# One decode block on one core: the second gate/up round and eight down row chunks in two whole loads, four single chunks at the end

## The chip, the core and the metric

The kernel runs on one core of one Trainium2 chip. The metric is the device time of one execution in microseconds (us), the median of several runs. In this document TensorE is the matrix engine (PE in the profile, its weight loads PEld), VectorE is DVE, ScalarE is ACT, GpSimd is POOL and SyncE is SP; SPq and ACTq are the queues from which SP and ACT issue transfers (DMAs).

## The reference

One token for each of eight sequences goes through an attention sublayer on cached keys and values and then through a gated feed-forward block, all in float32:

```python
W = 1024                                   # last W of 4096 cached positions
q = layernorm(x) @ wq                      # x: 8 x 1024, 32 heads of 128
p = softmax(q . k * 128 ** -0.5)           # 4 key/value heads, 8 query heads each
h = x + (p . v) @ wo
n = layernorm(h)
out = h + (gelu(n @ w_gate) * (n @ w_up)) @ w_down     # 1024 -> 3584 -> 1024
```

All weights and the cache window are read once: some 111 MB.

## The kernel before

All weights pass through one SBUF region, `space`, of 128 KB per partition, seen as two buffers `wbuf[0]` and `wbuf[1]` of 64 KB per partition each (8192 KB over 128 partitions). The loads alternate between the buffers: two for wq, two for the keys, two for the values, two for wo, then the gate and up weights. Every load is one DMA, issued by SP in program order through `move` (line 91) with the semaphore of the last matmul that still reads the place. SP waits in order, so an issue that waits holds back every issue behind it.

Each weight matrix is used with a batch of 8 on the narrow side. A matmul takes 32 stationary columns (four copies of the 8 rows) against 512 moving columns, and its result goes to 32 of the 128 PSUM partitions; the four partition quarters are the four **column groups** j, and matmuls on different groups run side by side. A float32 matmul appears in the trace as two records, each with its weight load.

The feed-forward block has two rounds, `SETS = (4, 3)`: round 0 covers 4 column groups of 512 of the 3584 hidden columns, round 1 the other 3. For each round k, s = 0 is the gate and s = 1 the up product (line 376): a loop over the eight 128-row slices c and, inside, over the groups j. After the gate ScalarE applies gelu (L386), after the up VectorE multiplies (`hm`, L389), TensorE transposes (L188, L397), and VectorE writes the transposed hidden rows to `at` (L400), from which the down product takes its stationary operand.

Round 0 loads into the two whole buffers. Round 1 has two loads of 6144 KB, which lie one behind the other at the front of `space`: the gate load waits for `used[0, 0]` (the end of round 0's gate products), the up load for `half_used` (half of round 0's up products). `place` and `base` are the end of them: 24 rows of 1024 per partition out of 32.

The down weights are 28 row chunks q of 128 x 1024. They come in `PARTS = (8, 8, 4, 4, 2, 1)` chunks per load and then the last one, 27, in two column pieces `ENDS = (128, 128)` of each quarter of 256. The first eight (4096 KB) go to the free quarter of `space` after `used[0, 1]`; chunks 8 to 15 and 16 to 19 wait for `used[1, 0]`, all others for `used[1, 1]`. Between these two issues stand the eight small `side` loads (line 436), which bring 320 columns of chunk 19 in another layout.

TensorE multiplies chunks pair by pair into `ya` (L461): two chunks by two halves of 512 columns on the four groups. Chunk pair 16 (`SLOW`) uses two groups only. `first = 28 - TAIL` is where this ends; with `TAIL = 2` it covers chunks 0 to 25. Then VectorE copies `ya` to `d1` (L474). Chunk 26 is multiplied in another form, by `add` (L483): each group takes one quarter of 256 output columns, in two halves in the banks `acc` and `tb`. After it `add` folds `d1` into the same banks with the constant `add2`. The two pieces of chunk 27 follow (L495), each as its load lands; ScalarE copies each half to `o_fin` (L498), and two DMAs write the result, one issued by SP and one by ACT.

Of the kernel before, what the change touches and what calls it, by code (L numbers as in the profile page):

```python
# [7 lines left out]
P = 128  # L8
B = 8
D = 1024  # L10
# [4 lines left out]
NC = D // P  # L15
# [3 lines left out]
N = 512  # L19
# [8 lines left out]
SIDE = 19  # L28
SIDE_COLS = 320
SIDE_ROWS = (0, 16, 64, 80)  # L30
ENDS = (128, 128)
TAIL = 2


SLOW = range(16, 18)
# [2 lines left out]
class Flow:  # L38
# [50 lines left out]
    def move(self, name, out, src, *waits, engine="sync"):  # L89
        s = self.sem(name)  # L90
        self.start(engine, lambda e: e.dma_start(out, src), waits).then_inc(s, 16)  # L91
        return s, 16


def decode_block(nc, x, wq, kt, v, wo, gu, dn, side, ends, outs):
# [14 lines left out]
    def sb(name, *shape):  # L110
        return nc.alloc_sbuf_tensor(name, list(shape), F32).ap()
# [243 lines left out]

    at = sb("at", P, DF // P, 32)
    at_ok = []
    q0 = 0  # L360
# [2 lines left out]
    for k, nb in enumerate(SETS):  # L363
        pair = big[1 - k].rearrange("p (s n) -> p s n", s=2)
        clear = (ps[1][1], h_ok)[k]
        for s in range(2):
            if k == 0:
                w, w_in, wb = load(gu[k][s], f"gu{k}_{s}", "c n", c=NC)
            else:
                n = NC * nb * N  # L370
                w = space[:, place:place + n].rearrange("p (c n) -> p c n", c=NC)
                w_in = move(f"gu{k}_{s}", w, gu[k][s], (used[0, 0], half_used)[s])
                place += n
            for c in range(NC):
                for j in range(nb):
                    tok = run("tensor", lambda e: e.matmul(  # L376
                        pair[32 * j:32 * j + 32, s, :], ht[c], w[:, c, j * N:(j + 1) * N],
                        start=(c == 0), stop=(c == NC - 1)),
                        w_in, ht_ok, clear, mark=(c in (NC // 2 - 1, NC - 1) and j == nb - 1))
                if (k, s, c) == (0, 1, NC // 2 - 1):  # L380
                    half_used = tok
            used[k, s] = tok
            if s == 0:
                rows = 32 * nb
                ge = sb(f"ge{k}", P, N)
                g_ok = run("scalar", lambda e: e.activation(  # L386
                    ge[:rows], pair[:rows, 0, :], AF.Gelu_apprx_tanh), tok)
        hm = sb(f"hm{k}", P, N)
        tok = run("vector", lambda e: e.tensor_mul(hm[:rows], ge[:rows], pair[:rows, 1, :]), tok, g_ok)  # L389
        hp, tok = transposes(ta, hm[:rows], N // P, tok, ta_free, rows)  # L390
        if k == 1:

            g, i = divmod(SIDE - q0, N // P)
            sp = ta[0:48, N - 32 * len(SIDE_ROWS):N].rearrange("p (s m) -> p s m", m=32)
            assert g == 0 and rows * (N // P) + 32 * len(SIDE_ROWS) <= N
            for s, c0 in enumerate(SIDE_ROWS):
                tok = run("tensor", lambda e: e.transpose(  # L397
                    sp[:, s, :], hm[0:32, i * P + c0:i * P + c0 + 48], ident[0:32, 0:32]),
                    mark=(s == len(SIDE_ROWS) - 1))
        ta_free = run("vector", lambda e: e.tensor_copy(  # L400
            at[:, q0:q0 + nb * (N // P), :].rearrange("p (j i) m -> p i j m", j=nb),
            hp.rearrange("p i (j m) -> p i j m", j=nb)), tok)
        at_ok.append(ta_free)
        if k == 1:
            at_side = sb("at_side", 48, len(SIDE_ROWS), 32)
            side_ok = run("scalar", lambda e: e.copy(at_side, sp), ta_free)
        q0 += nb * (N // P)
# [11 lines left out]
    def rows_of(q):  # L419
        return ring[:, slot(q)]  # L420

    arrived = {}
    q0 = 0
    for i, n in enumerate(PARTS):


        a, b = slot(q0), slot(q0) + n
        clear = used[0, 1] if a >= base else used[1, 0] if b * D <= place // 2 else used[1, 1]
        assert b <= SLOTS and (a >= base or b <= base)
        if q0 <= SIDE < q0 + n:  # L430
            assert SIDE == q0 + n - 1

            side_in = fl.sem("w_side")
            for h, src in enumerate(side):
                p0 = h % 4 + 32 * (h // 4)
                fl.start("sync", lambda e: e.dma_start(w_side[p0:p0 + 13:4], src), [zero[-1]]).then_inc(
                    side_in, 16)
            side_in = side_in, 16 * len(side)
            here = move(f"wd{i}", space[:, a * D:b * D - SIDE_COLS], dn[i], clear)
        else:  # L440
            here = move(f"wd{i}", ring[:, a:b], dn[i], clear)
        arrived.update((q, here) for q in range(q0, q0 + n))
        q0 += n
# [35 lines left out]
    def add(lhs, rhs, *waits, start=False):  # L479

        for d_ps, a, b in halves:
            for j in range(NQ):
                run("tensor", lambda e: e.matmul(  # L483
                    d_ps[32 * j:32 * j + 32, :], lhs(j), rhs(j)[:, a:b], start=start, stop=False),
                    *waits, mark=False)

    for q in range(first, last):
        add(lambda j: at[:, q, :], lambda j: rows_of(q)[:, j * QW:(j + 1) * QW], arrived[q], at_ok[1],
            start=(q == first))
    add(lambda j: add2[:, j // 2, :], lambda j: d1[:, (j % 2) * QW:(j % 2) * QW + QW], d1_ok)  # L490
    o_fin = sb("o_fin", P, QW)
    done = []
    for (c0, n, t, here), (d_ps, a, b) in zip(blocks, halves):
# [107 lines left out]
```

## Time and profile before

| | |
|---|---|
| median of 3 runs | 265.2 us (265.1 to 265.26) |
| the profiled execution, whole | 265.43 us |
| its span in the trace | 264.1 us |
| mean granted TensorE clock | 0.774 of full speed |
| TensorE matmuls busy | 139.8 us, 53% of the span |
| VectorE, ScalarE, GpSimd busy | 23.3, 10.9 and 5.5 us |
| DMA | 111.44 MB, mean 422 GB/s |

Times in the rows are us from the start of the span unless marked ns. A row of the timeline gives start and length of a merged group, engine, line, operation, output and inputs with their shape, the count, and in brackets the idle time of that engine before it and what ended it. A row of the chain of waits gives start, length and what ran or was waited for. In tables by stretch the columns are the stretch, its length, busy time and count of PE, PEld, DVE, ACT and POOL, the granted TensorE clock (1.00 is 2.4 GHz, 0.50 is 1.2 GHz), the busy share of the 16 DMA engines and GB/s. In a list of DMA issues the last number is the time from issue to landing.

### The profile page before, as it was taken

The page shows a single profiled execution, that of the slowest core. Times are in us where ns is not written, and L with a number is a line of the kernel's source. Part 1 is how long each engine was busy: PE and PEld are TensorE (multiplying, and loading weights), DVE is VectorE, ACT ScalarE, POOL GpSimd, SP SyncE. Part 2 cuts the span into 40 slices and gives each one's busy share as a digit, 9 for nine tenths or more (in the row PEclk, how much of TensorE's full clock was granted, in tenths as well). Part 3 has the DMA queues.
Part 4 walks back from the last instruction along what each step waited for, and adds up shares of the span by engine and source line. Part 5 has one row for each costly group of instructions (what it writes and reads, how often), then busy time and mean ns, then how long its engine had stood idle before and what let it go on. Part 6 is the DMA issues. An engine that isn't in the chain of part 4 may idle for free.

```text
span 264.1 us, 2071 instructions
## 1 busy us (share of the span) xinstructions
PE 139.8 (53%) x958; PEld 40.4 (15%) x958; DVE 23.3 (9%) x55; ACT 10.9 (4%) x17; POOL 5.5 (2%) x15
## 2 busy tenths in 40 slices
PE   0015805805905806806707808818509677587596
PEld 0011201201201301302202202112102111122122
DVE  0320100100020110200200100160000200010001
ACT  1010000000010010110000000020000000000000
POOL 8000000000000000000000000000000000000000
PEclk9999985985865975975955956965955959599599
DMA  8997999999799989989998999999999989999995
GB/s 318 481 457 338 476 476 390 407 467 477 328 476 467 439 367 457 469 347 477 447 457 367 479 437 437 397 437 477 390 407 439 477 387 442 412 442 432 402 413 191
DMA packets 3256, 111.44 MB, mean 422 GB/s; under 512 B 392, under 2 KB 648, under 8 KB 1072
## 3 DMA queue, kind: packets, MB, share of 16 engines
q1 hardware_dynamic: 3088, 111.22, 98.0%
q8 instruction: 7, 0.11, 0.2%
q10 hardware_dynamic: 160, 0.10, 0.1%
q14 instruction: 1, 0.01, 0.0%
HBM read 111.18 MB, written 0.13 MB: 422 GB/s over the span
## 4 chain that ended last, share of the span: by engine, by line
DMA 78%; PE 20%; SPq 0%; issue 0%; ACT 0%
DMA w<-gu 20%; DMA w<-wq 16%; DMA w<-v 11%; DMA w<-kt 11%; DMA w<-wo 11%; DMA w<-dn 9%; PE big L376 6%; PE tb L233 4%; PE tb L308 4%; PE ya L336 3%; PE big L261 3%; SPq L91 0%; PE acc L483 0%; ACT o_fin L498 0%; PE tb L483 0%
## 5 line engine op out<-in xcount | busy, mean ns | idle before, releaser
L376 PE MATMUL big<-w,ln_t 128*32 128x512 f32 x224 | 37.8, 758 | 19.8 <-DMA w<-gu 19.8
L336 PE MATMUL ya<-w,ot 128*32 128x512 f32 x128 | 18.9, 755 | 18.8 <-DMA w<-wo 18.8
L261 PE MATMUL big<-w,qz 128*32 128x512 f32 x128 | 18.0, 724 | 19.3 <-DMA w<-kt 19.3
L461 PE MATMUL ya<-w,at 128*32 128x512 f32 (+1 forms) x104 | 16.1, 695 | 4.6 <-DMA w<-dn 4.6
L376 PEld LDWEIGHTS big<-w,ln_t 128*32 128x32 f32 x224 | 9.2, 135 | 47.0 <-issue 26.7
L308 PE MATMUL tb<-w,pt 128*32 128x512 f32 x64 | 9.5, 757 | 9.4 <-DMA w<-v 9.4
L233 PE MATMUL tb<-w,ln_t 128*32 128x512 f32 x64 | 9.5, 762 | 8.9 <-DMA w<-wq 8.9
L308 PE MATMUL acc<-w,pt 128*32 128x512 f32 x64 | 8.9, 719 | 10.0 <-DMA w<-v 10.0
L233 PE MATMUL acc<-w,ln_t 128*32 128x512 f32 x64 | 8.9, 720 | 7.5 <-DMA w<-wq 7.5
L188 PE MATMUL ta<-ident,ln_xn 64*128 64x64 f32 x16 | 2.2, 318 | 19.4 <-DVE ln_xn L214 19.4
L336 PEld LDWEIGHTS ya<-w,ot 128*32 128x32 f32 x128 | 5.2, 135 | 31.0 <-issue 31.0
L261 PEld LDWEIGHTS big<-w,qz 128*32 128x32 f32 x128 | 4.7, 130 | 31.9 <-issue 22.3
L389 DVE TENSOR_TENSOR hm<-ge,big 128x512 f32<-128x512 f32 (+1 forms) x2 | 1.4, 686 | 56.7 <-PE big L376 56.7
L461 PEld LDWEIGHTS ya<-w,at 128*32 128x32 f32 x104 | 3.8, 124 | 15.7 <-issue 8.7
L270 DVE TENSOR_REDUCE nmax<-big 128x1 f32<-128x1024 f32 x2 | 2.4, 1224 | 33.9 <-PE big L261 33.9
L272 ACT ACTIVATE p<-big,nmax 128x1024 f32<-128x1024 f32 x2 | 2.2, 1114 | 76.6 <-DVE nmax L270 76.6
L308 PEld LDWEIGHTS tb<-w,pt 128*32 128x32 f32 x64 | 2.6, 134 | 15.6 <-issue 15.6
L188 PEld LDWEIGHTS ta<-ident,ln_xn 64*128 64x128 f32 x16 | 1.9, 216 | 20.3 <-DVE ln_xn L214 20.3
L308 PEld LDWEIGHTS acc<-w,pt 128*32 128x32 f32 x64 | 2.5, 130 | 15.8 <-issue 15.8
L233 PEld LDWEIGHTS tb<-w,ln_t 128*32 128x32 f32 x64 | 2.3, 135 | 15.5 <-DMA w<-wq 9.1
L233 PEld LDWEIGHTS acc<-w,ln_t 128*32 128x32 f32 x64 | 2.5, 130 | 13.2 <-issue 13.2
L205 ACT ACTIVATE ln_sd<-ln_ve 64x1 f32<-64x1 f32 x2 | 0.4, 203 | 69.4 <-DVE ln_ve L204 69.4
(81 smaller groups left out, 53.3 us busy)
## 6 DMA issues: line engine op xcount, KB each, us to landing
w<-gu SPq DMA_DIRECT2D x2, 6144.0 KB, 23.5
w<-dn SPq DMA_DIRECT2D x2, 4096.0 KB, 26.6
w<-dn SPq DMA_DIRECT2D x1, 2048.0 KB, 19.9
w<-dn SPq DMA_DIRECT2D x1, 1888.0 KB, 23.6
w<-dn SPq DMA_DIRECT2D x1, 1024.0 KB, 22.0
w<-dn SPq DMA_DIRECT2D x1, 512.0 KB, 22.7
w<-ends SPq DMA_DIRECT2D x2, 256.0 KB, 23.0
w_side<-side SPq DMA_DIRECT2D x8, 20.0 KB
```

The source lines that it names most:

```text
L188: tok = run("tensor", lambda e, i=i: e.transpose(t[:, i, :], src[:, i * P:(i + 1) * P], ident[:rows, :rows]), id_ok, ready, clear, mark=(i ...
L205: tok = run("scalar", lambda e: e.activation(sd, ve, AF.Sqrt), tok)
L233: tok = run("tensor", lambda e, c=c, j=j: e.matmul(q_ps[32 * j:32 * j + 32, :], xt[c], w[:, c, j * N:(j + 1) * N], start=(c == 0), stop=(c ...
L261: tok = run("tensor", lambda e: e.matmul(s_ps[32 * r:32 * r + 32, k0:k0 + N], qz[hf][:, s, c0:c0 + 32], k_t[:, s, half * HB + b, k0:k0 + N ...
L270: tok = run("vector", lambda e: e.tensor_reduce(out=nmax, in_=s_ps, axis=AX.X, op=ALU.max, negate=True), tok)
L272: p_ok = run("scalar", lambda e: e.activation(p_sb, s_ps, AF.Exp, bias=nmax, accum_out=tot), tok)
L308: tok = run("tensor", lambda e: e.matmul(o3[32 * r:32 * r + 32], pt[:, c, 32 * r:32 * r + 32], v_t[:, s, c, half * HB:(half + 1) * HB, :], ...
L336: tok = run("tensor", lambda e: e.matmul(ya[32 * r:32 * r + 32, :], ot[:, 2 * hf * REP + h + e2].rearrange("p r b -> p (r b)"), w[:, h + e ...
L376: tok = run("tensor", lambda e: e.matmul(pair[32 * j:32 * j + 32, s, :], ht[c], w[:, c, j * N:(j + 1) * N], start=(c == 0), stop=(c == NC ...
L389: tok = run("vector", lambda e: e.tensor_mul(hm[:rows], ge[:rows], pair[:rows, 1, :]), tok, g_ok)
L461: tok = run("tensor", lambda e: e.matmul(ya[32 * r:32 * r + 32, 0:n], at[:, q + e2, :], rows_of(q + e2)[:, ch * N:ch * N + n], start=(q == ...
```

## The change

Round 1 and the first eight down chunks are laid out together in DRAM, 128 KB per partition, as [gate | up | chunks 0 to 7], and loaded by two DMAs of 8192 KB, `whole[0]` into `wbuf[0]` after `used[0, 0]` and `whole[1]` into `wbuf[1]` after `used[0, 1]`. `whole[0]` holds the gate weights and the first eight of the 24 (c, j) blocks of up: all of c = 0 and 1, and j = 0, 1 of c = 2. `whole[1]` holds the other 16 and the eight chunks. Every place in `space` stays what it was. `half_used` and the separate load of chunks 0 to 7 are gone. A product of round 1 now waits for the whole load in which its block lies.

The order of round 1's products changes. The gate goes over all three groups for c = 0 to 3, over groups 0 and 1 for c = 4 to 7, and then over c = 4 to 7 on group 2. The up products of c = 0 to 2 go group by group, the others as before; the ninth of them, (2, 2), is the first that needs `whole[1]`.

`TAIL` becomes 4: the pairs in `ya` end with chunk 23, and chunks 24, 25 and 26 are multiplied in the form of `add`. The copy to `d1` follows chunk 23, and the fold of `d1` stands ahead of chunk 24. `ENDS` becomes (160, 96). All loads from chunk 8 on keep their sizes, order and waits, except the two pieces of chunk 27.

```diff
-ENDS = (128, 128)
-TAIL = 2
+ENDS = (160, 96)
+TAIL = 4
...
+    def order(k, s):
+        if (k, s) == (1, 1):
+            return [(c, j) for j in range(3) for c in range(3)] + \
+                [(c, j) for c in range(3, NC) for j in range(3)]
+        if (k, s) == (1, 0):
+            return [(c, j) for c in range(NC) for j in range(3 if c < NC // 2 else 2)] + \
+                [(c, 2) for c in range(NC // 2, NC)]
+        return [(c, j) for c in range(NC) for j in range(SETS[k])]
...
-                w_in = move(f"gu{k}_{s}", w, gu[k][s], (used[0, 0], half_used)[s])
+                if s == 0:
+                    whole = [move(f"whole{i}", wbuf[i], src, used[0, i]) for i, src in enumerate(gu[k])]
                 place += n
...
+            for c, j in order(k, s):
+                if k == 1:
+                    w_in = whole[(place - n + (c * nb + j) * N) // BUF]
+                tok = run("tensor", lambda e: e.matmul(
+                    pair[32 * j:32 * j + 32, s, :], ht[c], w[:, c, j * N:(j + 1) * N],
+                    start=(c == 0), stop=(c == NC - 1)),
+                    w_in, ht_ok, clear, mark=((c, j) == order(k, s)[-1]))
...
-    arrived = {}
-    q0 = 0
-    for i, n in enumerate(PARTS):
+    q0 = SLOTS - base
+    arrived = {q: whole[1] for q in range(q0)}
+    for i, n in enumerate(PARTS[1:], 1):
...
-        clear = used[0, 1] if a >= base else used[1, 0] if b * D <= place // 2 else used[1, 1]
+        clear = used[1, 0] if b * D <= place // 2 else used[1, 1]
...
+    add(lambda j: add2[:, j // 2, :], lambda j: d1[:, (j % 2) * QW:(j % 2) * QW + QW], d1_ok,
+        start=True)
     for q in range(first, last):
-        add(lambda j: at[:, q, :], lambda j: rows_of(q)[:, j * QW:(j + 1) * QW], arrived[q], at_ok[1],
-            start=(q == first))
-    add(lambda j: add2[:, j // 2, :], lambda j: d1[:, (j % 2) * QW:(j % 2) * QW + QW], d1_ok)
+        add(lambda j: at[:, q, :], lambda j: rows_of(q)[:, j * QW:(j + 1) * QW], arrived[q], at_ok[1])
```

## Rows read from the trace of the kernel before

**Rows 1.** Page, DMA queues: packets, MB, share of 16 engines over the span

```profile
q1 hardware_dynamic: 3088, 111.22, 98.0%
```

**Rows 2.** Chain of waits in time: start, length, what it was

```profile
90.58 30.26 DMA w<-v
...
130.45 29.14 DMA w<-wo
...
168.62 29.89 DMA w<-gu
...
205.10 22.48 DMA w<-gu
...
237.56 22.74 DMA w<-dn
```

**Rows 3.** Timeline of TensorE and its weight loads, round 1

```profile
213.09 9.46 PE L376 MATMUL big<-w,ln_t 128*32 128x512 f32 x48 [3.08 <-DMA w<-gu]
...
218.52 0.12 PEld L376 LDWEIGHTS big<-w,ln_t 128*32 128x32 f32 x3 [0.31 <-issue]
...
227.62 9.02 PE L376 MATMUL big<-w,ln_t 128*32 128x512 f32 x48 [5.08 <-DMA w<-gu]
```

**Rows 4.** Timeline of TensorE, ahead of the second layernorm

```profile
169.47 1.90 PE L347 MATMUL big<-y_sb,to_rows 128*64 128x512 f32 x4 [0.90 <-DVE y_sb L344]
```

**Rows 5.** Timeline of SP, the issues around the change

```profile
222.98 5.08 SPq L436 DMA_DIRECT2D w_side<-side  x8
228.10 9.89 SPq L91 DMA_DIRECT2D w<-dn  x4
238.03 0.91 SPq L91 DMA_DIRECT2D w<-ends  x2
```

**Rows 6.** Stretches of 1 us: busy times, granted clock, DMA share, GB/s

```profile
204.00:205.00 1.00, 1.00 (x12) 0.24 (x8) 0.00 (x0) 0.00 (x0) 0.00 (x0) 0.85 0.23 98
...
224.00:225.00 1.00, 0.00 (x0) 0.00 (x0) 0.00 (x0) 0.00 (x0) 0.00 (x0) 0.89 0.34 147
231.00:232.00 1.00, 1.00 (x9) 0.31 (x6) 0.00 (x0) 0.00 (x0) 0.00 (x0) 0.70 1.22 524
245.00:246.00 1.00, 0.00 (x0) 0.00 (x0) 0.00 (x0) 0.00 (x0) 0.00 (x0) 0.63 0.99 415
```

**Rows 7.** Timeline of TensorE, down chunks 0 to 23

```profile
238.70 4.01 PE L461 MATMUL ya<-w,at 128*32 128x512 f32 x30
...
247.05 8.69 PE L461 MATMUL ya<-w,at 128*32 128x512 f32 x48 [4.34 <-DMA w<-dn]
...
255.66 1.27 PE L470 MATMUL ya<-w_side,at_side 48*32 48x320 f32 x8
...
256.86 1.92 PE L461 MATMUL ya<-w,at 128*32 128x512 f32 x16
```

**Rows 8.** List of DMA issues: KB each, us from issue to landing

```profile
w<-dn SPq DMA_DIRECT2D x1, 1888.0 KB, 23.6
...
w<-ends SPq DMA_DIRECT2D x2, 256.0 KB, 23.0
...
out<-o_fin ACTq DMA_DIRECT2D x1, 64.0 KB, 1.6
```

**Rows 9.** Timeline of all engines, the end

```profile
260.22 0.69 DVE L474 COPY d<-ya 128x512 f32<-128x512 f32 x1 [21.33 <-PE ya L461]
...
260.97 0.43 PE L483 MATMUL acc<-d,add 128*32 128x128 f32 x8
...
261.65 0.40 PE L495 MATMUL tb<-w,at 128*32 128x128 f32 x8
...
262.12 0.27 ACT L498 COPY o_fin<-tb 128x128 f32<-128x128 f32 x1
...
262.41 0.35 ACTq L91 DMA_DIRECT2D out<-o_fin  x1
```

**Rows 10.** Stretch of 1 us while the result is written, columns as above

```profile
263.00:264.00 1.00, 0.00 (x0) 0.00 (x0) 0.00 (x0) 0.00 (x0) 0.00 (x0) 1.00 0.44 131
```

More of the change, by code (lines that the diff above doesn't have):

```diff
@@ L371, in decode_block @@
                 w = space[:, place:place + n].rearrange("p (c n) -> p c n", c=NC)
-                w_in = move(f"gu{k}_{s}", w, gu[k][s], (used[0, 0], half_used)[s])
+                if s == 0:
+                    whole = [move(f"whole{i}", wbuf[i], src, used[0, i]) for i, src in enumerate(gu[k])]
                 place += n
[L374 to L381, printed above, removed]
+            for c, j in order(k, s):
[5 more added lines that the diff above has]
+                    w_in, ht_ok, clear, mark=((c, j) == order(k, s)[-1]))
             used[k, s] = tok
@@ L420, in rows_of @@
         return ring[:, slot(q)]
-    arrived = {}
-    q0 = 0
-    for i, n in enumerate(PARTS):
+    q0 = SLOTS - base
+    arrived = {q: whole[1] for q in range(q0)}
+    for i, n in enumerate(PARTS[1:], 1):
         a, b = slot(q0), slot(q0) + n
-        clear = used[0, 1] if a >= base else used[1, 0] if b * D <= place // 2 else used[1, 1]
-        assert b <= SLOTS and (a >= base or b <= base)
+        clear = used[1, 0] if b * D <= place // 2 else used[1, 1]
+        assert b <= base
         if q0 <= SIDE < q0 + n:
@@ L540 @@
     for nb in SETS:
-        for m in (B_w_gate, B_w_up):
-            gus.append(m[:, f0:f0 + nb * N].reshape(NC, P, nb * N).transpose(1, 0, 2).reshape(-1))
+        gus.append([m[:, f0:f0 + nb * N].reshape(NC, P, nb * N).transpose(1, 0, 2).reshape(P, -1)
+                    for m in (B_w_gate, B_w_up)])
         f0 += nb * N
@@ L545 @@
     at = [sum(PARTS[:i]) for i in range(len(PARTS))]
+    both = np.concatenate(gus[1] + [rows[:PARTS[0]].transpose(1, 0, 2).reshape(P, -1)], 1)
+    gus[1] = [both[:, :NC * SET], both[:, NC * SET:]]
     width = [n * D - (SIDE_COLS if a <= SIDE < a + n else 0) for a, n in zip(at, PARTS)]
@@ L548 @@
         rows[a:a + n].transpose(1, 0, 2).reshape(P, -1)[:, :m].reshape(-1)
-        for a, n, m in zip(at, PARTS, width)])
+        for a, n, m in list(zip(at, PARTS, width))[1:]])
     side = np.stack([
@@ L562 @@
         "x": own(A_x).reshape(B, D), "wq": own(wq), "kt": own(kt), "v": own(v), "wo": own(wo),
-        "gu": np.concatenate(gus), "dn": dn, "side": own(side), "ends": ends,
+        "gu": np.stack([own(g) for k in gus for g in k]), "dn": dn, "side": own(side), "ends": ends,
     }
@@ L577 @@
     flat, f0 = aps["dn"], 0
-    aps["dn"] = []
-    for n, m in zip(PARTS, width):
+    aps["dn"] = [None]
+    for n, m in list(zip(PARTS, width))[1:]:
         t = flat[f0:f0 + P * m]
@@ L584 @@
     aps["side"] = [aps["side"][i] for i in range(8)]
-    flat, f0 = aps["gu"], 0
-    aps["gu"] = []
-    for nb in SETS:
-        size = P * NC * nb * N
-        aps["gu"].append([
-            flat[f0 + i * size:f0 + (i + 1) * size].rearrange("(p c n) -> p c n", p=P, c=NC)
-            for i in range(2)
-        ])
-        f0 += 2 * size
+    aps["gu"] = [[aps["gu"][2 * k + i] for i in range(2)] for k in range(2)]
+    aps["gu"][0] = [g.rearrange("p (c n) -> p c n", c=NC) for g in aps["gu"][0]]
     decode_block(nc, outs=outs, **aps)
```

## Prediction, written before the changed kernel ran

> **What bounds the kernel now.** I read the DMA queues first. The one queue that carries the weights occupies the 16 DMA engines for 98.0% of the span [rows 1], while TensorE is busy for 53%. Then I read the chain of waits in time, because a share over the whole span doesn't tell which wait ends last. There each load takes over where the one before ended: landings (start plus length) at 120.84, 159.59 and 198.51, each after two loads of 8192 KB, at 227.58 after two of 6144 KB, and at 260.30 [rows 2]. Matmuls appear on this chain only in the time in which the next load was running anyway. So the kernel is a stream of loads with a short tail: the last piece of chunk 27 lands at about 238.5 + 23.0 = 261.5 [rows 5, 8], and the span ends at 264.1. A change can gain in three ways: bytes move faster, the tail behind 261.5 gets shorter, or a place where the stream ran dry is filled. It loses if TensorE or a late issue falls behind the stream.
>
> **Two loads in place of three.** The bytes stay the same, so only a cost per load can be saved. Two 8192 KB loads took 38.75 and 38.92 us, two 6144 KB loads 29.07 us [rows 2]; three quarters of the former are 29.06 to 29.19. A fixed cost per load is therefore nil as far as these rows can tell. Chunks 0 to 15 (two loads of 4096 KB) took 247.05 - 227.58 = 19.47 us up to the matmuls that waited for them [rows 2, 7], as one load of 8192 KB does. The three loads thus took 29.07 + 9.73 = 38.80, and two whole ones would take 38.75 to 38.92: a gain of 0.05 to a loss of 0.12. I take 0.
>
> **Are the loads issued in time?** `whole[0]` waits as the gate load did. `whole[1]` waits for all of round 0's up products rather than half: these start at 198.56, and sixteen record rounds of 0.43 us, the first 5.7 us of them at half clock, end them at 208.3 (the clock was half until 204.3, see below). It is needed when `whole[0]` has landed, 198.51 + 19.4 = 217.9, so 9 us are in hand. `whole[1]` lands at 237.3. Before, chunks 8 to 15 were issued just ahead of 222.98, where the side loads begin on SP [rows 5]; they wait for the end of the gate products, which moves (next part) to 230.2 to 231.1, 6 us before they are needed. Behind that wait on SP stand eight side issues (5.08 us), chunks 16 to 19 and then the wait for the up products (next part: 242.4) with chunks 20 to 27 behind it. Chunk 19 lands at 228.10 + 23.6 = 251.7 [rows 5, 8], so these have 9 us in hand too. All of it is hidden; were one cover gone, the price would be the lateness plus at most the 1.6 us that a small transfer took from issue to landing [rows 8].
>
> **Round 1 on TensorE.** With full clock a record of 512 columns takes 0.12 + 0.31 = 0.43 us per group [rows 3], so a product (two records) takes 0.86, for up to four groups side by side; at half clock twice that. Four records in a row on the same groups with changing weights took 1.90 us, that is 4 x 0.43 and a drain of some 0.2 [rows 4]: work on one group costs time in proportion and no more. Where the clock stands I read from stretches of 1 us: 0.85 in the one from 204 puts a rise at 204.3, 5.7 us after the products began at 198.56; 0.70 from 231 puts one at 231.6, 4.0 us after 227.62 [rows 3, 6]. Falls: 0.89 from 224 is a fall at 224.8, 2.2 us after matmuls ended (222.55); 0.63 from 245 is one at 245.3, 2.55 us after 242.71 [rows 3, 6, 7].
>
> The gate goes from 8 steps of 0.86 to 12: four on three groups, four on two, four on one. Starting at 217.9 with a clock that rises after 4.0 to 5.7 us, it takes 12 x 0.86 + 2.0 to 2.85 = 12.3 to 13.2 us and ends at 230.2 to 231.1 (before: 9.46). The eight up products from `whole[0]` go group by group; where one group's last meets the next group's first they overlap, so they make 6 steps, 5.1 us, to 235.3 to 236.2. TensorE then idles 1.1 to 2.0 us until 237.3. That is less than the 2.2 and 2.55 us after which the clock was seen to fall, so I expect the other 16 up products at full clock: one alone and five steps of three, 5.1 us, to 242.4. Before, the up products ended at 236.64; from there multiply, transposes, and chunks 0 to 7 ended at 242.71, 6.07 us later [rows 3, 7]. So these end at 248.5. Chunks 8 to 15 (since 247.05) take four steps, 3.4 us, to 251.9; before, they began at half clock. Pair 16 on two groups 1.71, pair 18 0.86 and the side products 1.27 [rows 7] end at 255.7. Before, the side products ended at 256.93 and chunks 20 to 23 began right there [rows 7]. Those have landed by 256.6 to 256.86; the row before doesn't show the landing, since TensorE was later, and I take 256.6. The reordering itself so costs nothing at the end: it lies in time in which TensorE had waited 5.08 and 4.34 us [rows 3, 7]. Without that cover its cost would be 6 steps, 5.1 us.
>
> **The tail.** Chunks 20 to 23 end at 256.6 + 1.92 = 258.5 [rows 7], the copy to `d1` (0.69, and 0.06 to start [rows 9]) at 259.3. Nothing of TensorE hides this copy now; before, chunk 26 did. Then come the fold and chunks 24, 25 and 26: a quarter-form chunk streams four records of a quarter length, 0.43 us, as a chunk in `ya` does, so these end at 259.3 + 4 x 0.43 = 261.05. Loads 24 to 26 (all in by 260.30 [rows 2]) don't hold them up. The 160-column piece of chunk 27 takes 0.27 to 261.3, and the 96-column piece then starts when it lands, at 261.5. Before, it started at 261.65, behind the fold that had waited for `d1` to 260.97 [rows 9]: 0.15 gained. Its matmuls stream 32 columns less, four records of 0.43 x 32/512 over two passes: some 0.05 of their 0.40; ScalarE's copy of 0.27 and its DMA lose about 0.03 together. The rest, copy, issue and 1.6 us of landing, stays. Sum: 0.15 + 0.05 + 0.03 = 0.23 us.
>
> The smaller write could cost instead: its rows are 384 B, where 512 B were. The engines were busy for 0.44 us with both halves [rows 10], so twice the time for one half is at most 0.2 us more. The Trainium skill (DMA: Bandwidth & Descriptors, Specifications) says that below 512 B a DMA engine reads, modifies and writes. By that rule the gain would be used up; no row here has such a write. I take 0 and keep 0.2 for the range.
>
> **The sum** is made against the profiled execution: 265.43 - 0.23 = 265.2. The median, 265.2, lies 0.23 under that execution, so a median of 265.0 is my forecast, with 264.8 to 265.3 for this case. About 0.2% (0.53 us) is what a measurement of this kernel can tell from no change.
>
> **Rivals.**
>
> *The clock falls in the gap before `whole[1]`.* The idle time of up to 2.0 us is close to 2.2. If the clock rises early, the first eight end early and the gap is longest. The remaining products and the chain behind them would then run partly at half clock: from about 237.4 until 4.0 to 5.7 us after 237.3, some 3.5 to 5.5 us, which costs 1.7 to 2.7. Chunks 20 to 23 would begin at 257.4 to 258.4 rather than 256.6. In the chain from there (1.92, 0.75, five steps to the last piece) nothing waits, so the last piece starts 0.5 to 1.5 later than before: 265.6 to 266.6 as a median, of which I take 265.7, since overlap of the side products with the next chunks shortens it. For it: every earlier pause fell to 0.50. Against it: those were all longer. Half of its cases stay within 0.2%.
>
> *One group doesn't keep the clock up (slower).* If the one-group stretch of the gate, from 226.7 on, and the eight up products don't hold the clock as four groups do, it falls 2 us or more into that stretch. The eight up products then take 10.3 us, to 241.3, past the landing of `whole[1]`, and the rest starts cold: up products to some 248.5 rather than 242.4, and after the 1 us in hand the end is up to 5 us later, 265.5 to 270, with 267.5 as the middle. It decides once the granted clock falls between 226 and 237. For it: no row shows a stretch of several us on one group. Against it: three groups let the clock rise at 231.6 as four did at 204.3 [rows 6], and the stretch with pair 16 on two groups ran on at full clock behind 252.
>
> *A saved load saves time (faster by more than 0.2%).* If each load had a fixed cost of about 2 us on the stream, one load less would give 263.0. The Trainium skill (DMA: Bandwidth & Descriptors, Anatomy of one DMA) puts such a fixed part of about 2.0 us on each DMA of another issuing path. Here the next load is queued long before the last ends, and rows 2 leave nothing of it.
>
> *The change does nothing that shows.* The last landing, the copies and the write decide, and 0.23 us goes in the 96-column write: 265.2.
>
> **How the numbers follow.** Forecast 0.47; clock falls in the gap 0.25; one group doesn't hold the clock 0.14; a saved load 0.04; nothing shows 0.10. Faster by over 0.2%: 0.05 (the saved load and a sliver of the forecast). Slower: 0.12 + 0.14 = 0.26. Within: 0.69. The range runs from 264.7 to 266.3: it leaves out the saved load and most of the one-group case, some 0.16.
>
> **What would show each step.** Landings of `whole[0]` and `whole[1]` near 217.9 and 237.3; the gate ending near 230.5; full clock from about 222 to 237 and beyond; the side products ending before 256.6; the fold starting near 259.3 and the last piece at its landing, 261.5. I am wrong if the clock drops before 237, if chunks 20 to 23 start later than 257, or if the stream ends before 261.3.

## Result and the profile after

| | before | changed |
|---|---|---|
| median | 265.2 us (6 runs, 265.1 to 265.31) | 266.62 us (6 runs, 265.93 to 267.11) |
| profiled execution, whole | 265.43 us | 266.54 us |
| its span | 264.1 us | 265.0 us |

The ratio is 1.005 with a 95% interval of 1.004 to 1.006: the change makes the kernel slower by half a per cent, where 265.0 had been forecast and a time above 266.3 had been left out. The executions of the changed kernel also spread over 1.2 us, those before over 0.2. Between the medians the loss is 1.42 us, between the two profiled executions 1.1; the traces account for the 0.9 by which their spans differ.

The chain of waits of the changed kernel, in time (start, length, what it was), the counterpart of [rows 2]:

```profile
208.20 28.83 DMA w<-gu
...
237.07 7.50 PE big L390 x32
...
247.16 9.44 PE ya L473 x75
```

Before, the chain ran over the loads to 260.30 [rows 2]. Now the last load on it lands at 237.03 (the second whole load; 208.20 + 28.83), and from there on TensorE alone carries it: up products, chunks, the copy to `d1`, the quarter steps, without any wait for data. TensorE has become the bound of the last 28 us. The last piece of chunk 27 lands at 261.4 (see the loads, below) and waits 1.1 us until TensorE takes it up at 262.51.

The timeline of TensorE, VectorE and ScalarE, for [rows 3, 7, 9]:

```profile
217.67 12.23 PE L390 MATMUL big<-w,ln_t 128*32 128x512 f32 x64 [7.99 <-DMA w<-gu]
...
228.13 0.59 ACT L398 ACTIVATE ge<-big 96x512 f32<-96x512 f32 x1 [39.20 <-PE big L390]
...
237.07 7.48 PE L390 MATMUL big<-w,ln_t 128*32 128x512 f32 x32 [7.17 <-DMA w<-gu]
...
246.59 10.01 PE L473 MATMUL ya<-w,at 128*32 128x512 f32 x78
...
256.53 1.27 PE L482 MATMUL ya<-w_side,at_side 48*32 48x320 f32 x8
...
257.73 1.92 PE L473 MATMUL ya<-w,at 128*32 128x512 f32 x16
...
259.72 0.69 DVE L486 COPY d<-ya 128x512 f32<-128x512 f32 x1 [12.95 <-PE ya L473]
...
260.47 0.48 PE L495 MATMUL acc<-d,add 128*32 128x160 f32 x8 [0.81 <-DVE d L486]
...
262.51 0.35 PE L507 MATMUL tb<-w,at 128*32 128x96 f32 x8
```

The timeline merges the gate and the eight up products of the first whole load into one row: they take 12.23 us and end at 229.90; the gate's gelu starts at 228.13. TensorE then waits 7.17 us. The other 16 up products take 7.48. Chunks 0 to 19 follow without a pause, the side products end at 257.80, chunks 20 to 23 start at 257.73 (256.86 before), and the last piece at 262.51 (261.65 before). That 0.86 us is the span's 0.9.

The granted clock in stretches of 1 us (the third number from the right), for [rows 6]:

```profile
220.00:221.00 1.00, 1.00 (x6) 0.19 (x3) 0.00 (x0) 0.00 (x0) 0.00 (x0) 0.52 1.66 721
230.00:231.00 1.00, 0.00 (x0) 0.00 (x0) 0.00 (x0) 0.00 (x0) 0.00 (x0) 1.00 1.51 655
234.00:235.00 1.00, 0.00 (x0) 0.00 (x0) 0.00 (x0) 0.00 (x0) 0.00 (x0) 0.80 0.68 295
236.00:237.00 1.00, 0.00 (x0) 0.00 (x0) 0.00 (x0) 0.00 (x0) 0.00 (x0) 0.50 1.22 524
241.00:242.00 1.00, 1.00 (x9) 0.28 (x6) 0.00 (x0) 0.00 (x0) 0.00 (x0) 0.78 1.14 492
```

It rises at 220.95 (0.52 in the first row), holds through the gate and the first up products, falls at 234.6, 4.7 us after they ended, and is at 0.50 when the second load lands. It rises again at 241.4, 4.4 us after the work began.

### The profile page after: what moved, and what is told of

It is laid out like the page before. It is cut to its first block, busy times and chain, and to the rows that moved or that the text cites. A ratio compares the mean times of both kernels' runs of the same rounds, so it can differ in the third digit from the quotient of the medians.

```text
span 265.0 us, 2118 instructions
## 1 busy us (share of the span) xinstructions
PE 137.5 (52%) x982; PEld 41.3 (16%) x982; DVE 23.3 (9%) x55; ACT 10.9 (4%) x17; POOL 5.5 (2%) x15
## 4 chain that ended last, share of the span: by engine, by line
DMA 71%; PE 27%; DVE 1%; issue 0%; ACT 0%; SPq 0%; DVEq 0%
DMA w<-gu 22%; DMA w<-wq 15%; DMA w<-kt 11%; DMA w<-wo 11%; DMA w<-v 11%; PE big L390 7%; PE ya L473 4%; PE big L261 4%; PE tb L233 4%; PE tb L308 4%; PE ya L336 3%; PE acc L495 0%; PE ya L482 0%; PE ya L465 0%; DVE d L486 0%
## 5 line engine op out<-in xcount | busy, mean ns | idle before, releaser
L390 PE MATMUL big<-w,ln_t 128*32 128x512 f32 x224 | 38.7, 745 | 27.3 <-DMA w<-gu 27.3
L261 PE MATMUL big<-w,qz 128*32 128x512 f32 x128 | 19.2, 766 | 19.8 <-DMA w<-kt 19.8
L390 PEld LDWEIGHTS big<-w,ln_t 128*32 128x32 f32 x224 | 9.9, 133 | 54.8 <-issue 27.5
L473 PE MATMUL ya<-w,at 128*32 128x512 f32 (+1 forms) x96 | 12.4, 589 | 0.0
L233 PEld LDWEIGHTS tb<-w,ln_t 128*32 128x32 f32 x64 | 2.3, 135 | 15.5 <-DMA w<-wq 9.3
L398 ACT ACTIVATE ge<-big 128x512 f32<-128x512 f32 (+1 forms) x2 | 1.2, 594 | 51.8 <-PE big L390 51.8
```

The costliest lines, as they stand in the source:

```text
L233: tok = run("tensor", lambda e, c=c, j=j: e.matmul(q_ps[32 * j:32 * j + 32, :], xt[c], w[:, c, j * N:(j + 1) * N], start=(c == 0), stop=(c ...
L261: tok = run("tensor", lambda e: e.matmul(s_ps[32 * r:32 * r + 32, k0:k0 + N], qz[hf][:, s, c0:c0 + 32], k_t[:, s, half * HB + b, k0:k0 + N ...
L390: tok = run("tensor", lambda e: e.matmul(pair[32 * j:32 * j + 32, s, :], ht[c], w[:, c, j * N:(j + 1) * N], start=(c == 0), stop=(c == NC ...
L398: g_ok = run("scalar", lambda e: e.activation(ge[:rows], pair[:rows, 0, :], AF.Gelu_apprx_tanh), tok)
L473: tok = run("tensor", lambda e: e.matmul(ya[32 * r:32 * r + 32, 0:n], at[:, q + e2, :], rows_of(q + e2)[:, ch * N:ch * N + n], start=(q == ...
```

## Experiments

**1. The tail alone.** The kernel before, with its three loads and its order of round 1.

```diff
-ENDS = (128, 128)
-TAIL = 2
+ENDS = (160, 96)
+TAIL = 4
...
+    add(lambda j: add2[:, j // 2, :], ..., d1_ok, start=True)
     for q in range(first, last):
-        add(..., start=(q == first))
-    add(lambda j: add2[:, j // 2, :], ..., d1_ok)
+        add(...)
```

> The kernel before with only the tail of the change: four single chunks, the fold ahead of them, pieces of 160 and 96 columns; three loads as before. Theory A (TensorE comes late and cold out of the gap ahead of the second whole load; the tail is no cause of its own): chunks 20 to 23 start at about 256.9 as before, end at 258.8, the copy to d1 at 259.55, and five quarter steps of 0.43 put the last piece at 261.6; span 263.9 to 264.1, median 265.0 to 265.3. Theory B (the copy to d1, which nothing on TensorE hides any more, costs the time by itself): the last piece starts 0.7 to 0.9 us later than 261.65, median 265.9 to 266.2.

Measured: 265.36 us (10 runs), before 265.24; ratio 1.0002 [0.9993, 1.0012]. The timeline of its end:

```profile
256.33 1.92 PE L461 MATMUL ya<-w,at 128*32 128x512 f32 x16
...
258.33 0.69 DVE L474 COPY d<-ya 128x512 f32<-128x512 f32 x1 [20.11 <-PE ya L461]
...
259.07 0.48 PE L483 MATMUL acc<-d,add 128*32 128x160 f32 x8 [0.81 <-DVE d L474]
...
261.30 0.37 PE L495 MATMUL tb<-w,at 128*32 128x96 f32 x8
```

Between 258.33 and 259.07 TensorE waits for the copy, and that costs nothing: four more steps follow, and the last piece starts at 261.30, when it has landed (261.26 in the trace). Theory B falls. The 0.23 us forecast for the tail don't show in the median either.

**2. The loads and the order alone**, with the tail of before.

```diff
-ENDS = (160, 96)
-TAIL = 4
+ENDS = (128, 128)
+TAIL = 2
```

and `add` for the fold behind chunk 26 again.

> The changed kernel with the tail of before: two whole loads and the new order of round 1, TAIL = 2, fold behind chunk 26, pieces of 128 and 128. Theory A: the up products still run partly at half clock from 237.1 to about 244.5, chunks 20 to 23 still start near 257.7 and end at 259.65; chunks 24 and 25 follow at once to 260.5, the copy ends at 261.25 beside chunk 26, fold 0.43, last piece at about 262.0 where the changed kernel had 262.51: span 264.4 to 264.6, median 265.8 to 266.2. So about half a microsecond of the loss would belong to the tail on top of a late TensorE. Theory B: back to 265.1 to 265.4.

Measured: 266.22 us (10 runs, 265.23 to 266.4); ratio 1.0027 [1.0014, 1.004].

```profile
236.92 7.92 PE L390 MATMUL big<-w,ln_t 128*32 128x512 f32 x32 [6.74 <-DMA w<-gu]
...
258.01 2.78 PE L473 MATMUL ya<-w,at 128*32 128x512 f32 x24
...
260.87 0.69 DVE L486 COPY d<-ya 128x512 f32<-128x512 f32 x1 [13.81 <-PE ya L473]
...
262.29 0.40 PE L507 MATMUL tb<-w,at 128*32 128x128 f32 x8
```

The up products start at half clock (7.92 us in all), TensorE is late at 258.01, and the last piece starts at 262.29. So the loads and the order make the kernel slower by themselves. The median lies just above the 265.8 to 266.2 of theory A, and the executions fall into two sets: three at 265.23 to 265.48, as before, and seven at 266.04 to 266.4, of which the profiled one (266.04) is one. Against the changed kernel this one is some 0.4 us faster at the median, and its trace is 0.5 us shorter from the start of chunk 20 to the last piece (258.01 to 262.29, there 257.73 to 262.51): with a late TensorE the copy to `d1`, here beside chunk 26, is no longer free in the new tail.

**3. The plain order of round 1** in the changed kernel.

```diff
     def order(k, s):
-        if (k, s) == (1, 1):
-            return ...
-        if (k, s) == (1, 0):
-            return ...
         return [(c, j) for c in range(NC) for j in range(SETS[k])]
```

> The changed kernel with round 1's products in the plain order, all groups inside every c, for gate and up. Theory A (matmuls on different groups run beside each other whatever their order, so the new order hardly lengthens the work): the products of the first whole load end at 228.5 to 229.5 where they ended at 229.9, the clock falls before 237, the up products end at 244 to 245, median 266.2 to 267.1, as the changed kernel. Theory C (the new order is itself the loss, because it delays the end of the gate or leaves groups idle): median below 266.0.

Measured: 266.4 us (5 runs, 265.85 to 267.15); ratio 1.0048 [1.0029, 1.0067], the changed kernel's.

```profile
217.72 11.24 PE L384 MATMUL big<-w,ln_t 128*32 128x512 f32 x64 [8.00 <-DMA w<-gu]
...
237.16 7.46 PE L384 MATMUL big<-w,ln_t 128*32 128x512 f32 x32 [8.21 <-DMA w<-gu]
```

The products of the first load end at 228.96 where they end at 229.90 with the new order, and the second load finds the clock low either way. Theory C, a median below 266.0, falls. The new order lengthened TensorE's work by 1 us, not by the 5 to 6 that the forecast gave it.

**4. Eight extra products on the idle fourth group** fill the gap. They write to `ya`, which is begun anew later.

```diff
             for c, j in order(k, s):
+                if (k, s, c, j) == (1, 1, 2, 2):
+                    for g in [3] * 8:
+                        run("tensor", lambda e: e.matmul(
+                            ya[32 * g:32 * g + 32, :], ht[0], w[:, 0, 0:N], start=True, stop=True),
+                            ya_free, mark=False)
```

> The changed kernel with eight extra products on the idle fourth column group, into the bank ya that is written anew later, between the last up product of the first whole load and the first of the second; they read data that is there and change nothing in the result. One of them takes 0.86 us at full clock, all 6.9. Theory A: TensorE is busy to 236 or later, the clock stays at 1.00, the up products take 5.1 to 5.6 us and end at 242.2 to 242.8 in place of 244.55, chunks 20 to 23 start when they have landed (256.5), the last piece at its landing (261.45): span 263.7 to 264.0, median 265.0 to 265.3. Rival (work on one group doesn't hold the clock): it falls before 237 in spite of the products, and the median stays at 266.3 or more.

Measured: 265.29 us (10 runs, 265.06 to 266.28); ratio 1.0011 [1.0001, 1.0022]; profiled span 263.8.

```profile
230.32 5.74 PE L390 MATMUL ya<-w,ln_t 128*32 128x512 f32 x13
...
237.29 5.34 PE L395 MATMUL big<-w,ln_t 128*32 128x512 f32 x32 [1.23 <-DMA w<-gu]
...
256.43 1.92 PE L478 MATMUL ya<-w,at 128*32 128x512 f32 x16 [0.56 <-DMA w<-dn]
```

and the clock in it:

```profile
235.00:236.00 1.00, 1.00 (x3) 0.11 (x1) 0.00 (x0) 0.00 (x0) 0.00 (x0) 1.00 0.08 33
236.00:237.00 1.00, 0.06 (x1) 0.00 (x0) 0.00 (x0) 0.00 (x0) 0.00 (x0) 1.00 1.14 492
```

TensorE works until 236.06, from 230.32 on with the extra products alone, on one group of four, and the clock stays at 1.00 through the remaining gap of 1.23 us. The up products take 5.34 us in place of 7.48, and chunks 20 to 23 wait for their load again. This is the loss of the changed kernel, taken back by nothing but a warm clock. The rival that one group doesn't hold the clock falls with it. Four of the ten executions still took 265.5 or more; experiments 8 and 9 are about these.

**5. The step in dispute, measured by itself:** sixteen extra products, four on each group, written group by group.

```diff
-                    for g in [3] * 8:
+                    for g in sorted(list(range(4)) * 4):
```

> The changed kernel with sixteen extra products at the same place, four on each column group, written group by group: four on group 0, then four on 1, 2 and 3. They go into ya and change nothing in the result. It measures the step on which the forecast's gap stood. In order, one group's run beside the next only where they meet (the forecast's reckoning): 13 steps of 0.86 us, 11.1 us, so TensorE is busy from 229.9 to about 241 and the up products of the second load start 4 us late. All groups beside each other whatever the order: 4 steps, 3.4 us, so it ends at about 233.3 and idles until 237. A queue of a few matmuls per group would lie between: 5 to 9 us.

Measured: one execution, 265.01 us, span 263.7.

```profile
228.79 0.59 PE L390 MATMUL ya<-w,ln_t 128*32 128x512 f32 x1
...
229.65 7.98 PE L390 MATMUL ya<-w,ln_t 128*32 128x512 f32 x30
```

The first starts at 228.79, the last ends by 237.63 (229.65 + 7.98): 8.8 us, between the 11.1 of strict steps and the 3.4 of free groups. The starts of the records in the trace tell how: each group's first record begins 1.75 us, four records, after the first of the group before, when that one has two products left. So in this order a group begins once the run ahead of it has two products to go, and a run of n products takes n - 2 steps, the last run n.

**6. Pair 16 on four groups.**

```diff
-SLOW = range(16, 18)
+SLOW = ()
```

> The changed kernel with chunk pair 16 on four column groups in place of two. Theory A (TensorE is late and every step behind the second load counts): pair 16 takes 0.86 in place of 1.71 us, chunks 20 to 23 start 0.8 us earlier, at 256.8 to 256.9, the last piece at 261.5 to 261.7; median 265.6 to 265.9 where the changed kernel had 266.62. If TensorE's lateness isn't the cause, no difference: 266.3 or more.

Measured: 265.61 us (10 runs, 264.98 to 266.22); ratio 1.0011 [1.0, 1.0021]. In the profiled execution (265.97):

```profile
247.10 9.15 PE L473 MATMUL ya<-w,at 128*32 128x512 f32 x78
```

The median falls by one microsecond for 0.86 us of TensorE time taken out behind the second load (9.15 in place of 10.01): it was on the path. In this execution the clock rose at 242.45, later than in the changed kernel's, so that the last piece started at 262.16 and not at the 261.5 to 261.7 expected.

**7. Nine extra products and pair 16 on four groups.**

> The changed kernel with nine extra products on the fourth column group (as eight before) and chunk pair 16 on four groups. Theory A: TensorE is busy until about 236.9, the clock holds in every execution, TensorE waits for chunks 20 to 23 by a microsecond or more, and the end is set by the last landing alone: median 265.0 to 265.2 with a spread of no more than the kernel before, 0.1 to 0.2 below it at best, since what lies behind the last landing is only some 0.2 us shorter. If the tail costs something of its own, it stays at 265.4 or more.

Measured: 265.31 us (12 runs, 264.88 to 268.37); ratio 1.0022 [0.9996, 1.0048]. The median lies 0.1 above the 265.0 to 265.2 expected and below the 265.4 of the other reading. The spread was not expected: four executions took 266.7 to 268.4. The profiled one (265.35) was not of these, so the trace doesn't show them:

```profile
256.31 1.93 PE L478 MATMUL ya<-w,at 128*32 128x512 f32 x16 [1.41 <-DMA w<-dn]
```

Here TensorE waited 1.41 us for chunks 20 to 23, and the granted clock stayed at 1.00 until after the end of the work. Two causes that the next experiments show could both act in the four, an eighth instruction load and a clock lost through this wait; which it was stays open.

**8. Four extra products** on the fourth group in place of the eight of experiment 4, with the tail of the change.

> The changed kernel with four extra products on the fourth column group in place of eight: they end at about 232.6 and leave a gap of 4.4 us ahead of the second load. Theory A: the clock falls in that gap in most executions (falls were seen 2.2 and 2.55 us after work had ended) and the time is that of the changed kernel or a little less, 266.0 to 266.8. If the mere presence of extra products helped, or one group's work counted in another way, the time would be half way or better, below 265.8.

Measured: 266.89 us (4 runs); ratio 1.0049 [1.0034, 1.0063]. The time is 0.1 above the expected range, and not for the expected reason alone. The clock fell at 236.5, just ahead of the load, and TensorE ended 0.8 us earlier than in the changed kernel (262.07 against 262.86). What took the time is the write of the result. The page's row of the instruction queue (packets, MB, share), and the issues of the write (KB, us to landing):

```profile
q8 instruction: 8, 0.13, 0.2%
```

```profile
out<-o_fin SPq DMA_DIRECT2D x1, 80.0 KB, 3.1
...
out<-o_fin ACTq DMA_DIRECT2D x1, 48.0 KB, 3.2
```

There are eight instruction loads here, seven before and in the changed kernel, and the write takes 3.1 and 3.2 us in place of 1.6 [rows 8]. The 16 more TensorE instructions of this kernel brought it. The packets in the trace show how it delayed the write: it ran from 263.26 to 264.43, and 16 of the write's 256 packets, the share of one of the 16 DMA engines, began only at 264.43, while all others were done by 263.77. So the run doesn't tell how much four products help. Experiments 4, 5 and 7 have eight loads too; in their profiled executions the additional one came between 260.8 and 262.6, ahead of the write, which took 1.6 to 2.0 us. Whether it came later in their slower executions isn't shown.

**9. Eight extra products with the tail of before**, whose stream has 48 TensorE instructions less: experiment 2 with the lines of experiment 4.

> Two whole loads and the new order of round 1 with the tail of before (as the second experiment), plus eight extra products on the fourth column group ahead of the second load. Its instruction stream is shorter than that of the experiments with extra products so far, in which an eighth instruction load appeared near 261 to 263; here seven are expected, and 1.6 us for the write of the result in every execution. Theory A: the clock holds to 237, chunks 20 to 23 wait for their landing (256.4), median 265.0 to 265.3, and no execution above 265.8. If executions of 266 and more remain, the clock still falls in some of them, or something else than the gap and the eighth load costs time.

Measured: 265.21 us (11 runs, 265.06 to 265.81), before 265.26; ratio 0.9998 [0.999, 1.0007]; seven instruction loads, 1.6 us for the write.

```profile
237.01 5.34 PE L395 MATMUL big<-w,ln_t 128*32 128x512 f32 x32 [0.71 <-DMA w<-gu]
...
256.32 1.92 PE L478 MATMUL ya<-w,at 128*32 128x512 f32 x16 [0.73 <-DMA w<-dn]
...
261.38 0.40 PE L512 MATMUL tb<-w,at 128*32 128x128 f32 x8
```

One execution touched 265.81; otherwise all are at the level of the kernel before. Whether the old tail or the missing eighth load took away the slower executions of experiment 4, this run doesn't separate. With a warm clock and seven instruction loads, whole loads are neither better nor worse than three.

**10. Nine extra products, pair 16 on four groups, pieces of 160 and 96, but `TAIL = 2`.**

> As the kernel with eight extra products and the tail of before, but nine extra products, chunk pair 16 on four column groups, and pieces of 160 and 96 columns. It takes from the changed kernel what should pay and leaves out the four single chunks. Theory A: TensorE is ahead of every load, the last piece starts at its landing and is 32 columns shorter: median 0.1 to 0.25 us below the kernel before. If what lies behind the last landing is what it was, or if the 384-byte rows of the smaller write cost time, no difference.

Measured: 265.48 us (12 runs, 265.26 to 266.3); ratio 1.0013 [1.0002, 1.0023]. That is above the kernel before, where 0.1 to 0.25 below it had been expected. Seven executions lie at 265.26 to 265.51, five at 266.04 to 266.3. In the profiled one (266.04), one of the five:

```profile
253.46 1.27 PE L487 MATMUL ya<-w_side,at_side 48*32 48x320 f32 x8
...
256.23 4.48 PE L478 MATMUL ya<-w,at 128*32 128x512 f32 x24 [1.50 <-DMA w<-dn]
```

```profile
256.00:257.00 1.00, 0.77 (x8) 0.33 (x12) 0.00 (x0) 0.00 (x0) 0.00 (x0) 0.77 0.97 401
```

Now TensorE is early: the side products end at 254.73, chunks 20 to 23 begin at 256.23, and the clock falls at 256.53 as they begin. The 24 records of chunks 20 to 25 take 4.48 us in place of the 2.78 of experiment 2. In this execution a saved step of TensorE turned into a pause, and the pause into a cold tail; in the one of experiment 7 a pause of 1.41 us at the same place did not. The smaller write (48 KB in rows of 384 B) landed in 1.7 us, the larger in 1.6: the doubt about short rows finds next to nothing.

**11. Four extra products with the tail of before.**

> Four extra products in place of eight, with the tail of before, so that no eighth instruction load comes. They end near 232.6, and TensorE idles 4.4 us until the second load. Theory A: the clock falls in that gap in most executions, the up products take 6.5 to 8 us in place of 5.3, chunks 20 to 23 start at 256.8 to 257.6, and the median lies at 265.5 to 266.3, between the kernel without extra products (266.22) and that with eight. The write takes 1.6 us again; if it takes 3 us as with four extra products and the new tail, the eighth instruction load was not its cause.

Measured: 265.8 us (10 runs, 264.89 to 266.43); ratio 1.0019 [1.0008, 1.003]; seven instruction loads, 1.6 us for both writes.

```profile
229.19 2.31 PE L390 MATMUL ya<-w,ln_t 128*32 128x512 f32 x5
...
237.09 7.41 PE L395 MATMUL big<-w,ln_t 128*32 128x512 f32 x32 [5.59 <-DMA w<-gu]
```

The extra products end at 231.50, a microsecond earlier than expected. A gap of 5.59 us and up products at 7.41: the clock fell, and the time lies between experiments 2 and 9. The long write of experiment 8 went with its eighth instruction load.

**12. The same gap closed by order alone**, with runs long enough by the rule of experiment 5.

```diff
-            return [(c, j) for j in range(3) for c in range(3)] + \
+            return [(0, 2), (1, 2)] + [(c, j) for j in range(2) for c in range(3)] + [(2, 2)] + \
                 [(c, j) for c in range(3, NC) for j in range(3)]
...
-            return [(c, j) for c in range(NC) for j in range(3 if c < NC // 2 else 2)] + \
-                [(c, 2) for c in range(NC // 2, NC)]
+            return [(c, j) for c in range(2) for j in range(3)] + \
+                [(c, j) for j in range(3) for c in range(2, NC)]
```

> The changed kernel with nothing added and only the order of round 1 changed again: the gate over all three groups for c = 0 and 1, then six products in a row on each group; the first up products on group 2, then 0, then 1. Theory A with what the products group by group have shown (the next group begins when the run before it has two products, four records, left; so a run of n products takes n - 2 steps and the last one n): gate 2 + 4 + 4 + 6 = 16 steps of 0.86, up 2 + 1 + 3 - 2 = 4 or so, with a clock that rises 2 to 6 us after 217.7 the gate ends at 232.4 to 234.3 and the eight up products at 235.9 to 237.8, against 228.1 and 229.9 in the changed kernel. The gap is then at most 1.2 us, the clock stays at 1.00, the other up products end by 242.5 to 243, the last piece starts at its landing, and the median is 265.0 to 265.3, 1.3 below the changed kernel, with no execution above 265.9. If runs on one group are beside each other more than that, the gap stays over 3 us and the median at 266 or more; if they take their full length, the eight up products end after 238 and the time lies in between.

Measured: 266.86 us (6 runs, 266.31 to 268.18); ratio 1.0072 [1.0053, 1.009]. The timeline of TensorE and of SP's issue of chunks 8 to 15, and a row of its chain:

```profile
217.97 24.70 PE L390 MATMUL big<-w,ln_t 128*32 128x512 f32 x96 [8.62 <-DMA w<-gu]
...
234.67 0.33 SPq L91 DMA_DIRECT2D w<-dn  x1
...
252.79 2.77 PE L473 MATMUL ya<-w,at 128*32 128x512 f32 x16 [0.66 <-DMA w<-dn]
...
262.62 0.37 PE L507 MATMUL tb<-w,at 128*32 128x96 f32 x8
```

```profile
242.70 14.86 DMA w<-dn
```

The theory of the gap is right: gate, up products and the landing of the second load join without a pause in one stretch of 24.70 us, which ends at 242.67. The rule for runs is right too: the gate ends at 234.7, 0.4 past the 232.4 to 234.3 expected, and 16 steps of 0.86 from 217.97, half of the 5.4 us up to the clock's rise at 223.41 and 0.2 for the drain give 234.6. The time is not as expected, for a reason that neither theory in the expectation had: the gate now ends so late that chunks 8 to 15, which wait for it, are issued at 234.67. In the trace's records of packets the last 16 of the second load, one for each DMA engine, end between 234.87 and 236.84, and the first of chunks 8 to 15 begins at 235.62. In the changed kernel, where the gate ended at 228.1, they ended from 234.93 on and the first of chunks 8 to 15 began at 234.94, without a pause. The stream ends about 1 us later: the last piece lands at 262.57, where it landed at 261.40 in the changed kernel, and TensorE takes it up at once, at 262.62. The second load had landed 0.26 us later (237.29). TensorE waits for chunks 16 to 19 and for 20 to 23 and can begin with the latter at 257.60, 20.3 us after that landing; in experiment 4 it waited for them too, and there it was 256.43 - 237.29 = 19.1. The profiled execution is the fastest of the six; why others took up to 268.18 isn't shown.

## Why the prediction was wrong

**The loads: right.** The second whole load landed at 237.03 (237.3 forecast) and the last piece, the second of two issues on SP, at 246.4 + 15.0 = 261.4, no later than before [rows 5, 8]:

```profile
245.92 0.91 SPq L91 DMA_DIRECT2D w<-ends  x2
```

```profile
w<-ends SPq DMA_DIRECT2D x1, 192.0 KB, 15.0
```

Whole loads gain nothing by themselves (experiment 9). The issues had the time in hand that was claimed: chunks 8 to 15 went out at 228.12, nine us ahead. Experiment 12 shows the price once that cover is gone: issued 0.2 us before the first engine was free, the stream ended about 1 us later, within the 1.6 us given for it.

**The order of round 1: wrong, and the step that decided.** The forecast counted 12 steps for the gate and 6 for the eight up products, 18 in all, because it let a group begin only where the run before it meets its end. The trace of the changed kernel shows otherwise already. Its weight loads, two groups up to here and a third joining:

```profile
224.03 0.11 PEld L390 LDWEIGHTS big<-w,ln_t 128*32 128x32 f32 x2 [0.32 <-issue]
224.46 0.15 PEld L390 LDWEIGHTS big<-w,ln_t 128*32 128x32 f32 x4 [0.32 <-issue]
```

The first product of the gate's run on group 2 alone starts at 224.47, while groups 0 and 1 have two products each to go. By the rule of experiment 5, counted in steps of 0.86 us: the stretches on three and two groups end at 8; the run of four on group 2 lasts from 6 to 10, the up products on group 0 from 8 to 11, those on group 1 from 9 to 12, and the two on group 2 from 10 to 12. Twelve steps are 10.3 us, and the half clock up to 220.95 adds 1.6: 11.9, and 0.2 for the drain, against 12.23 measured. The missing 6 steps are 5.1 us, and they went straight into the gap: 7.17 us where 1.1 to 2.0 had been forecast. With 18 steps and the clock as it rose here, the work would have ended at about 235.0 (an estimate: 217.67 + 15.5 + 1.6 + 0.2) and the gap would have been 2.1 us.

**The clock in the gap: wrong because of that.** The forecast let the other 16 up products run at full clock in 5.1 us; they took 7.48, since the clock had fallen in the gap. The rival that it falls there had the chance 0.25 and is what happened. Its price was about right: 0.5 to 1.5 us for the last piece, 0.86 measured in the profiled execution. But the rival was sized at 265.7, from the lower end of its own price, and the range cut at 266.3; the median of the runs is 266.62. Even the forecast's own gap of up to 2.0 us was no safe cover. The two falls read from before, 2.2 and 2.55 us after work [rows 6], were not the earliest in that trace. Two others, in stretches of 1 us:

```profile
132.00:133.00 1.00, 0.00 (x0) 0.00 (x0) 0.63 (x2) 0.00 (x0) 0.00 (x0) 0.81 0.45 197
211.00:212.00 1.00, 0.00 (x0) 0.00 (x0) 0.00 (x0) 0.00 (x0) 0.00 (x0) 0.56 0.23 98
```

The first is a fall at 132.6, 2.0 us after TensorE's last work (130.66); the second one at 211.1, 1.1 us after four transposes that ended at 210.01 and 2.7 us after the up products of round 0. In experiment 10 the clock fell 1.8 us after work.

**The chain behind the second load: right, step by step.** From the end of the up products at 244.55, 12.04 us were forecast for multiply, transposes and chunks 0 to 19 (6.07 + 3.4 + 1.71 + 0.86): measured to 256.60, 12.05. Side products 1.27, chunks 20 to 23 1.92, copy 0.69, steps of 0.43: all as forecast, from a start 2.15 us later.

**The tail: right in mechanism, too small to see.** Experiment 1 ran as the forecast's tail did, the last piece at its landing, at 261.30; the ratio is 1.0002, and its interval (0.9993 to 1.0012) just leaves out the gain of 0.09% that had been forecast. The bare copy, which cost the forecast nothing at the end, does cost some 0.4 to 0.5 us once TensorE is late (experiment 2 against the changed kernel).

**The rival that one group doesn't hold the clock: wrong.** Experiment 4 held 1.00 from 230.3 to 236.1 on one group.

**Short rows.** The Trainium skill (DMA: Bandwidth & Descriptors, Specifications) says that a DMA engine does read-modify-write below 512 B. The traces show no price of it: the 48 KB in rows of 384 B landed 1.6 to 1.7 us after the issue in the changed kernel and in experiment 10, the 64 KB in rows of 512 B in 1.6 before [rows 8].

What stays open: why executions of the changed kernel differ by 1.2 us. That the moments of the clock's fall and rise differ from one execution to the next fits. No two executions of one kernel were traced, but up to the landing of the first whole load the changed kernel and the kernels made from it (experiments 2 to 12) do the same work, and there their twelve traces show a rise 3.0 to 5.6 us after the up products of round 0 had begun and a fall 1.0 to 4.2 us after the last transposes. Behind it, the traces of the kernels with a cold start (the changed kernel and experiments 2, 3, 6, 8 and 11) show falls 2.3 to 5.2 us after the work on the first load had ended and rises 2.9 to 5.4 us after the second load's had begun. That the 1.2 us come from this isn't shown. The slow executions of experiments 4, 7 and 12 are open too.

## What to carry to other kernels

When TensorE waits for loads, reckon each pause ahead of a burst: a change that moves work behind a later landing leaves a longer pause in front of it, and the burst starts at half clock just when it has become longer. Spreading products over fewer column groups stretched the work here only beyond the two products that each group takes in advance, so such a stretch is to be measured before it is counted on, and what waits for the stretched work (here the next load) has to be moved with it. No version here beats the kernel before: it takes up the last piece 0.1 us behind its landing, and the versions whose stream was on time and whose clock stayed up do no more than that (last piece at 261.44 in experiment 4 and 261.38 in 9, within 0.1 us of its landing).

## What was unexpected of the hardware

- Matmuls on a free column group start while the run before them, on another group, has two products (four records of 0.43 us) to go: 1.75 us from group to group for runs of four products (experiment 5).
- Work on a single column group holds the granted clock at 2.4 GHz for 5.7 us (experiment 4).
- The granted clock fell as little as 1.0 us after TensorE's last work where that was four transposes (209.68 to 210.71, changed kernel), 1.8 us in experiment 10, and as much as 5.4 us after a burst of 9.2 us (188.27 to 193.65, changed kernel). A pause of 1.50 us lost it (experiment 10), one of 1.41 us at the same place did not (experiment 7).
- Sixteen more TensorE instructions brought an eighth instruction load. It ran for 1.17 us just as the result was written, one engine's share of the write began behind it, and the write took 3.1 to 3.2 us in place of 1.6 (experiment 8).
